# A planner for a fused attention and mixer kernel: one server for all DMAs, the weights' subtraction on DVE, and more of the work planned

## The chip, the core and the metric

The kernel runs on one core of a Trainium2 chip. A core has five engines that run side by side: TensorE (PE in the profile; its weight loads are PEld), VectorE (DVE), ScalarE (ACT), GpSimd (POOL) and SyncE (SP), which here only issues DMAs. Each engine works through its own instructions in the order in which they were written, and waits at one whose inputs or buffers aren't ready. The metric is the device time of one execution in microseconds.

## The reference

```python
scores = cap * np.tanh(scale * np.matmul(q, k.transpose(0, 1, 3, 2)) / cap)
attn = np.exp(scores - np.max(scores, axis=-1, keepdims=True))
attn = attn / (np.sum(attn, axis=-1, keepdims=True) + 1e-09)
x = np.matmul(attn, v)          # 4 batches, 12 heads, 448 tokens, 64 per head
x = x.transpose(0, 2, 1, 3).reshape(4, 448, 768)
h = np.maximum(x.transpose(0, 2, 1) @ w_tok1, 0.0) @ w_tok2      # 448 -> 256 -> 448
u = x + h.transpose(0, 2, 1)
out = u + np.maximum(u @ w_ch1, 0.0) @ w_ch2                     # 768 -> 1536 -> 768
```

The weights come as 64-bit floats, everything else as 32-bit floats.

## The kernel before

**Attention.** The heads are taken in pairs (24 pairs, 6 for each batch), and a pair in units: three blocks of 128 keys each, and the last 64 keys of two pairs together. A unit's scores are a product into bank pair ps_qk, ACT takes tanh (L334) and exp (L342) of them into a tile e, and a second product adds e times v to bank ps_pv. DVE adds the e tiles up (acc, L403, L410, L420). For two pairs at a time, a quad, PE sums acc over the keys (ps_s, L432); the sums go through SBUF (xs), four small DMAs (sums), a reciprocal on DVE (L471), a DMA to memory (rs) and four broadcasting DMAs (rb), and DVE multiplies the unscaled result by rb (L499) into u.

**Token mixing.** A half batch at a time: PE transposes u (ps_t, L508); ACT and DVE split the result in a high and a low part (L515, L518, L519); PE multiplies with w_tok1 (ps_h, 11 matmuls a tile, L536); ACT and DVE take the relu and split it (L542, L545); PE multiplies with w_tok2 (ps_u, 6 matmuls a tile, L559), and DVE adds it to u (L565). The tiles ps_s, ps_t, ps_h and ps_u share a ring of two banks, "c".

**Channel mixing.** u is split in high and low parts (ACT L655, DVE L656). For 6 groups of 256 of the 1536 channels and for each batch, `ch1` makes ps_g (36 matmuls, L771), whose relu is split by ACT (L779) and DVE (L780) into g; `ch2` makes six tiles ps_o (6 matmuls each, L796), and DVE adds each to u (L801). The tiles ps_o lie in rings "b" and "c" by turns.

**Weights.** A chunk of 512 columns is loaded as 64-bit numbers (wraw, L194, two buffers) and turned into a high and a low part: ACT takes a scaled absolute value (L212), DVE builds the 32-bit number from the bits (L218, L219, L225, L226), ACT rounds the high part (L235), and POOL subtracts it to get the low part (L239). Token weights are 4 chunks, each group of channel weights is 6, 36 in all; two sets of buffers alternate between groups.

**The order.** The order of the instructions on every engine is set by a planner that runs while the program is built. A `Job` has an engine, a cost (how long the engine is taken), a time to its result, and what it waits for; `Plan` gives each engine the job whose inputs are ready first, plus a slack by which less urgent work steps back. PE's own time is `plan.pe`. Token mixing is cut in steps that `background` puts between the attention units, a fixed quota of time after every second unit. DMAs are jobs on "sp" with a fixed time to landing each. Splits of u, the relu of `ch1` and the additions of `ch2` are written out in place, and the plan's clocks are moved along by hand. From the end of attention on, in `open_m1`, the hand-made order is closed.

## Time and profile before

| | |
|---|---|
| median of 3 runs | 605.88 us (605.72 to 608.96) |
| profiled execution, its time | 607.8 us |
| its span, first to last instruction | 605.7 us |
| mean granted clock of TensorE | 0.997 of 2.4 GHz |
| PE busy | 594.7 us |
| DVE busy | 388.0 us |
| ACT busy | 254.0 us |
| POOL busy | 57.6 us |

A busy time is the union of an engine's instructions. For PE it is no measure of how near it is to its peak, since matmuls overlap and their ends are modelled; what PE loses shows in its waits and in the clock that it was granted.

### The profile page before, as it was taken

How to read it: one execution, taken by the hardware profiler on the slowest of the kernel's cores; microseconds unless marked ns; L12 is line 12 of the kernel's file. 1: busy time of each engine (PE TensorE's matmuls, PEld its weight loads, DVE VectorE, ACT ScalarE, POOL GpSimd, SP SyncE). 2: the span in 40 equal slices, each digit the busy share in tenths (PEclk: the TensorE clock that was granted, in tenths of full speed). 3: DMA queues.
4: the chain of work that ended last, by engine and by line, in shares of the span. 5: the costliest groups of instructions: out<-in, count | busy, mean ns of one | idle time of the engine just before them, and what ended most of it. 6: DMA issues, size and time to landing. Idle time of an engine off the chain costs nothing.

```text
span 605.7 us, 7785 instructions
## 1 busy us (share of the span) xinstructions
PE 594.7 (98%) x3012; PEld 439.4 (73%) x3012; DVE 388.0 (64%) x626; ACT 254.0 (42%) x330; POOL 57.6 (10%) x48
## 2 busy tenths in 40 slices
PE   8999989999999999999999999999999999999997
PEld 2333434544454468888998999899999999999986
DVE  2999799967756787769685386437643753333324
ACT  7999877959685862342321022012211220000000
POOL 0201002110000000022310022002200120000000
PEclk9999989999999999999999999999999999999999
DMA  7534564414332023012323022202120200000224
GB/s 236 181 95 154 163 191 133 138 46 123 82 118 83 25 87 102 1 41 65 111 97 104 1 63 55 92 0 77 65 69 1 69 1 1 1 1 4 106 80 180
DMA packets 24621, 49.13 MB, mean 81 GB/s; under 512 B 6784, under 2 KB 16512, under 8 KB 24576
## 3 DMA queue, kind: packets, MB, share of 16 engines
q1 hardware_dynamic: 24288, 48.37, 25.5%
q8 instruction: 25, 0.41, 0.3%
q14 instruction: 20, 0.16, 0.1%
q10 hardware_dynamic: 288, 0.18, 0.1%
HBM read 42.86 MB, written 5.59 MB: 80 GB/s over the span
## 4 chain that ended last, share of the span: by engine, by line
PE 81%; DVE 12%; DMA 3%; issue 2%; ACT 2%; POOL 0%; SPq 0%; DVEq 0%; ACTq 0%; POOLq 0%
PE ps_o L796 27%; PE ps_g L771 25%; PE ps_pv L382 9%; PE ps_qk L312 8%; PE ps_u L559 3%; PE ps_h L536 3%; DVE wz L225 2%; PE ps_s L432 2%; DMA rb<-rs 2%; PE ps_qk L318 2%; PE ps_pv L385 1%; PE ps_t L508 1%; DVE wz L226 1%; DVE wz L219 1%; DVE uhl L656 1%
## 5 line engine op out<-in xcount | busy, mean ns | idle before, releaser
L796 PE MATMUL ps_o<-g,wc 128*128 128x448 f32 x864 | 181.8, 367 | 1.3 <-DVE u L801 1.0
L796 PEld LDWEIGHTS ps_o<-g,wc 128*128 128x128 f32 x864 | 161.5, 188 | 17.4 <-DVE u L801 2.5
L771 PE MATMUL ps_g<-uhl,wc 128*128 128x448 f32 x648 | 137.1, 367 | 0.0
L771 PEld LDWEIGHTS ps_g<-uhl,wc 128*128 128x128 f32 x648 | 121.1, 188 | 10.4
L801 DVE TENSOR_TENSOR u<-u,ps_o 128x448 f32<-128x448 f32 (+1 forms) x145 | 86.4, 613 | 46.3 <-PE ps_o L796 46.2
L334 ACT ACTIVATE e<-ps_qk,tsc 128x896 f32<-128x896 f32 x84 | 81.0, 1014 | 32.5 <-PE ps_qk L312 27.9
L239 POOL TENSOR_TENSOR wc<-wz,wc 128x512 fp32r<-128x512 f32 x36 | 49.3, 1372 | 396.5 <-ACT wc L235 371.3
L342 ACT ACTIVATE e<-e,near 128x896 f32<-128x896 f32 x84 | 84.4, 1051 | 0.0
L779 ACT ACTIVATE g<-ps_g 128x896 fp32r<-128x896 f32 x24 | 22.0, 915 | 144.8 <-PE ps_g L771 144.8
L780 DVE SCALAR_TENSOR_TENSOR g<-ps_g,g 128x896 fp32r<-128x896 f32 x24 | 26.1, 1088 | 74.4 <-ACT g L779 74.4
L312 PE MATMUL ps_qk<-qkraw 64*128 64x448 f32 x288 | 67.1, 575 | 0.2 <-DMA qkraw<-in_qk 0.2
L382 PE MATMUL ps_pv<-e,vn 128*64 128x448 f32 x288 | 64.9, 564 | 1.0 <-ACT e L342 1.0
L235 ACT ACTIVATE wc<-wz 128x512 fp32r<-128x512 f32 x36 | 22.6, 628 | 84.4 <-DVE wz L226 36.4
L312 PEld LDWEIGHTS ps_qk<-qkraw 64*128 64x128 f32 x288 | 24.4, 189 | 43.4 <-issue 18.2
L771 PE MATMUL ps_g<-last_u,wc 128*128 128x448 f32 x216 | 45.1, 366 | 1.4 <-issue 1.4
L771 PEld LDWEIGHTS ps_g<-last_u,wc 128*128 128x128 f32 x216 | 40.5, 188 | 5.2 <-issue 1.8
L212 ACT ACTIVATE wz<-wraw 128x512 f32<-128x512 f32 x36 | 24.1, 672 | 44.4 <-DMA wraw<-in_wc 25.1
L218 DVE TENSOR_SCALAR wz<-wz 128x512 f32<-128x512 f32 (+1 forms) x40 | 17.0, 428 | 38.0 <-ACT wz L212 37.9
L382 PEld LDWEIGHTS ps_pv<-e,vn 128*64 128x64 f32 x288 | 17.0, 137 | 32.6 <-issue 18.6
L403 DVE TENSOR_TENSOR acc<-e 128x896 f32<-128x896 f32 x24 | 26.2, 1091 | 19.0 <-ACT e L342 18.8
L420 DVE TENSOR_TENSOR acc<-acc,e 64x448 f32<-64x448 f32 x48 | 32.8, 683 | 6.4 <-ACT e L342 5.1
L536 PEld LDWEIGHTS ps_h<-wc,last_u 128*128 128x128 f32 x176 | 30.3, 188 | 9.0 <-issue 6.0
(50 smaller groups left out, 432.3 us busy)
## 6 DMA issues: line engine op xcount, KB each, us to landing
wraw<-in_wc SPq DMA_DIRECT2D x36, 512.0 KB, 3.5
qkraw<-in_qk SPq DMA_DIRECT2D x23, 448.0 KB, 3.6
vn<-in_v SPq DMA_DIRECT2D x24, 224.0 KB, 2.6
rb<-rs SPq DMA_DIRECT2D x48, 112.0 KB, 2.9
out_t<-u SPq DMA_DIRECT2D x23, 224.0 KB, 1.9
wraw<-in_w SPq DMA_DIRECT2D x2, 512.0 KB, 5.6
wraw<-in_w SPq DMA_DIRECT2D x2, 448.0 KB, 4.3
sums<-xs SPq DMA_DIRECT2D x48, 1.8 KB, 1.8
```

The costliest lines, as they stand in the source:

```text
L239: nc.gpsimd.tensor_tensor(lo, bits(held["z"]), hi, op=ALU.subtract)
L312: nc.tensor.matmul(ps[:, j, :S], raw[r, 1, c * P:(c + 1) * P], raw[r, 0], start=True, stop=True)
L334: nc.scalar.activation(e, ps[:, :, :S], AF.Tanh, scale=tsc)
L342: nc.scalar.activation(e, e, AF.Exp, scale=near)
L382: nc.tensor.matmul(o, vn[x % 3][:, j * NF + c], es[b, p, c][:, j], start=first, stop=last)
L403: nc.vector.tensor_tensor(accs[b, q][0][:, i], es[b, p, 0], es[b, p, 1], op=ALU.add)
L420: nc.vector.tensor_tensor(t, t, es[b, p - i, NF][r, i], op=ALU.add)
L536: nc.tensor.matmul(ps[:, :HALF], w, x, start=(n == 0), stop=(n == len(mm) - 1))
L771: nc.tensor.matmul(ps[:, i, :S], w[:, wi, cc, fs], uhl[b][:, ui, cc, :], start=(n == 0), stop=(n == 3 * NC - 1))
L780: nc.vector.scalar_tensor_tensor(g[:, 1], ps[:, :, :S], 0.0, g[:, 0], op0=ALU.max, op1=ALU.subtract)
L796: nc.tensor.matmul(ps[:, :S], w[:, wi, i, cs], g[:, gi, i, :], start=(n == 0), stop=(n == 3 * GF - 1))
L801: nc.vector.tensor_tensor(u[b][:, cc, r], u[b][:, cc, r], ps[:, r], op=ALU.add)
```

## The change

The planner's DMA jobs become transfers through one server: each has a size, the server works them off one after the other in the order of issue, at `BYTE` ns per byte, and a transfer lands `LANDING` ns after the server is done with it. The loads of the first channel weights get starting times that rise along the chunks. The subtraction of every decoded chunk goes from POOL to DVE. Splits of u, relu of `ch1` and additions of `ch2` become jobs of the plan; `ch2` takes a bank from the ring that comes free first; the first group's products are placed by a loop of their own (`first_group`) among what is left of token mixing; the quota of background work that wasn't used is kept for later, up to twice the quota; later groups' weights step back further (slack 60000 for 3000).

```diff
+LANDING = 1270
+BYTE = 3.8 / 1024
+STAGGER = 26.0
+SHARE = 7.0
+SPLIT = 2000.0
+SMALL = 8 * 1024
...
         at, e, j = n
         self.jobs[e].remove(j)
         self.free[e] = at + j.cost
-        j.end = at + j.took
+        if e == "sp":
+            self.bus = max(self.bus, self.free[e]) + j.took * BYTE
+            j.end = self.bus + LANDING
+        else:
+            j.end = at + j.took
         j.emit()
...
-            held["wz"].read(job("pool", 1400, 1400, last, (*key, 4), slack=slack, key=key))
+            held["wz"].read(job("dve", 530, 620, last, (*key, 4), slack=slack, key=key))
 
         def last():
-            nc.gpsimd.tensor_tensor(lo, bits(held["z"]), hi, op=ALU.subtract)
+            nc.vector.tensor_tensor(lo, bits(held["z"]), hi, op=ALU.subtract)
...
-        l = job("sp", 434, 3700, load, room("wraw"), since, slack=slack)
+        l = job("sp", 434, 8 * P * n, load, room("wraw"), since, slack=slack)
...
-        job("sp", 373, 3600, lambda: load_pair(b, p), room("raw"), slack=1500.0, key=("raw", b, p))
+        job("sp", 373, 8 * P * S, lambda: load_pair(b, p), room("raw"), slack=1500.0, key=("raw", b, p))
...
-        job("sp", 638, 2900, lambda: bring(0), m, room("rb"))
+        job("sp", 638, 8 * D * S, lambda: bring(0), m, room("rb"))
...
-    w0, w0_steps = group_weights(0, slack=20000.0, since=60000.0)
+    w0, w0_steps = group_weights(0, slack=20000.0, since=65000.0, stagger=STAGGER)
...
-        background(TOK / 7)
+        credit = min(credit + QUOTA, 2 * QUOTA)
+        credit -= background(credit)
...
-    def split_u(b, cc):
+    def split_u(b, slack=0.0):
...
+            job("act", 468, 568, high, ("u", b, cc), plan.pe, slack=slack, key=("uh", b, cc))
+            job("dve", 536, 620, low, ("uh", b, cc), slack=slack, key=("split", b, cc))
...
+        hold.read(job("act", 891, 918, high, plan.pe + DRAIN, slack=-500.0, key=("gh", g, b)))
+        hold.read(job("dve", 1010, 1092, low, ("gh", g, b), slack=-500.0, key=("g", g, b)))
...
-            pool, tag = ((ps_b, "b"), (ps_c, "c"))[cc % 2]
-            ps = pool.tile([P, 512], F32, tag=tag, name="ps_o")
+            clear(lambda: rings["b"].room() is None and rings["c"].room() is None)
+            n, tag = min((free_at(tag), tag) for tag in ("b", "c"))
+            plan.pe = max(plan.pe, n)
+            ps = (ps_b if tag == "b" else ps_c).tile([P, 512], F32, tag=tag, name="ps_o")
...
-            hold.read(plan.inline("dve", 530, 612))
+            hold.read(job("dve", 530, 612, lambda cc=cc, ps=ps: add_out(b, cc, ps, last), plan.pe + DRAIN))
...
+    def first_group(w):
+        started, g, at = 2, [], []
+        while len(g) < B:
+            if opened and started == 2:
+                started = 3
+            if started == 3 and not any(left):
+                done["tok",] = plan.pe
+                order.close()
+                split_tile(B - 1, None)
+                split_u(B - 1, -500.0)
+                started = B
+            n, m = len(g), len(at)
+            t = plan.ready([("split", n, 0)]) if n < started and n - m < 2 else None
+            if t is not None and t <= plan.pe + PATIENCE:
+                g.append(ch1(w[0], n))
+            elif m < n and (t := plan.ready([("g", 0, m)])) is not None and t <= plan.pe + PATIENCE:
+                ch2(w[1], m, g[m], False)
+                at.append(plan.pe)
+            elif not chunk():
+                rest()
+            fill()
```

What this does to the order is seen in three places. The first is SP's queue where the rb of batch 0's third quad are issued (line numbers differ, since the change adds lines: L194 is now L205, L286 is L298, L291 is L303, L462 is L477, L489 is L504). Before:

```order
L475 DMA rs<-sums 128x14
L291 DMA vn_96<-in_v 128x448
L194 DMA wraw<-in_wc 128x1024 x2
L286 DMA qkraw<-in_qk 128x896
L489 DMA rb<-rs 64x1x448 x4
L462 DMA sums<-xs 32x1x14 x4
```

Now:

```order
L490 DMA rs<-sums 128x14
L303 DMA vn_96<-in_v 128x448
L504 DMA rb<-rs 64x1x448 x4
L298 DMA qkraw<-in_qk 128x896
L205 DMA wraw<-in_wc 128x1024
L477 DMA sums<-xs 32x1x14 x4
L490 DMA rs<-sums 128x14
L504 DMA rb<-rs 64x1x448 x4
```

The q/k load and the weight load have moved behind the four rb, one weight load has gone from here altogether, and the next quad's sums, rs and rb follow.

The second place is DVE at the end of token mixing, where the last batch's u (u_78) is split into last_u while batch 1's additions of ps_o to u_76 begin. Before:

```order
L565 TENSOR_TENSOR u_78<-u_78,ps_u 128x448
L656 TENSOR_TENSOR last_u<-u_78,last_u 128x448 x3
L780 SCALAR_TENSOR_TENSOR g<-ps_g,g 128x896
L801 TENSOR_TENSOR u_76<-u_76,ps_o 128x448 x2
L656 TENSOR_TENSOR last_u<-u_78,last_u 128x448
L801 TENSOR_TENSOR u_76<-u_76,ps_o 128x448
```

Now:

```order
L581 TENSOR_TENSOR u_78<-u_78,ps_u 128x448
L676 TENSOR_TENSOR last_u<-u_78,last_u 128x448 x5
L237 SCALAR_TENSOR_TENSOR wz<-wraw,wz 128x512
L250 TENSOR_TENSOR wc_1_81<-wz,wc_1_81 128x512
L250 TENSOR_TENSOR wc_1_82<-wz,wc_1_82 128x512
L815 SCALAR_TENSOR_TENSOR g<-ps_g,g 128x896
L844 TENSOR_TENSOR u_76<-u_76,ps_o 128x448 x2
```

All splits now come ahead of the relu's low part (L815), together with two of the subtractions that were POOL's (L250).

The third place is PE in the first third of attention, at the second quad's sums (ps_s) and at the first token products (ps_h). Before, with other attention units left out between the two pieces:

```order
L312 MATMUL ps_qk<-qkraw 128x448 x4
L432 MATMUL ps_s<-acc,ones 32x448 x4
L382 MATMUL ps_pv<-e,vn_96 64x448 x2
...
L432 MATMUL ps_s<-acc,ones 32x448 x4
L536 MATMUL ps_h<-wc_1_81,last_u 128x384 x11
L382 MATMUL ps_pv<-e,vn_97 64x448 x4
L312 MATMUL ps_qk<-qkraw 128x448 x4
L536 MATMUL ps_h<-wc_1_81,last_u 128x384 x11
```

Now:

```order
L324 MATMUL ps_qk<-qkraw 128x448 x4
L394 MATMUL ps_pv<-e,vn_96 64x448 x2
L397 MATMUL ps_pv<-e,vn_96 64x448 x2
L397 MATMUL ps_pv<-e,vn_97 64x448 x2
L324 MATMUL ps_qk<-qkraw 128x448 x4
L445 MATMUL ps_s<-acc,ones 32x448 x4
L524 MATMUL ps_t<-ident,u_75 128x128 x4
...
L445 MATMUL ps_s<-acc,ones 32x448 x4
L552 MATMUL ps_h<-wc_1_81,last_u 128x384 x22
```

The sums have moved behind the next products and stand directly before a transpose; the 22 token products stand in one piece.

## Rows read from the trace of the kernel before

**Rows 1.** The page, busy time of the engines: us (share of the span) xinstructions
```profile
PE 594.7 (98%) x3012; PEld 439.4 (73%) x3012; DVE 388.0 (64%) x626; ACT 254.0 (42%) x330; POOL 57.6 (10%) x48
```
**Rows 2.** Who PE waited for: us in total, times, longest us
```profile
PE ps_t L508 <- DVE wc L545: 1.5, 1, 1.5
PE ps_g L771 <- issue: 1.4, 1, 1.4
PE ps_pv L382 <- ACT e L342: 1.0, 2, 0.9
PE ps_o L796 <- DVE u L801: 1.0, 1, 1.0
...
PE ps_h L536 <- DVE wc L519: 0.5, 1, 0.5
PE ps_u L559 <- DVE wc L519: 0.4, 1, 0.4
PE ps_o L796 <- DVE wc L519: 0.3, 1, 0.3
```
**Rows 3.** Stretches: length, busy PE, PEld, DVE, ACT, POOL, granted clock, DMA share, GB/s
```profile
20.00:40.00 20.00, 20.00 (x108) 5.70 (x106) 19.47 (x32) 20.00 (x23) 4.41 (x3) 1.00 0.48 151
...
80.00:82.00 2.00, 2.00 (x8) 0.57 (x8) 1.95 (x4) 2.00 (x4) 0.00 (x0) 0.54 1.02 280
82.00:84.00 2.00, 2.00 (x8) 0.69 (x6) 1.53 (x3) 0.24 (x1) 0.00 (x0) 0.61 1.02 286
```
**Rows 4.** Timeline of SP's queue from 63 us: start, length, instruction
```profile
63.93 0.81 SPq L194 DMA_DIRECT2D wraw<-in_wc  x2
64.80 0.42 SPq L286 DMA_DIRECT2D qkraw<-in_qk  x1
65.26 2.82 SPq L489 DMA_DIRECT2D rb<-rs  x4
```
**Rows 5.** DMA issues: count, KB each, median us from issue to landing
```profile
wraw<-in_wc SPq DMA_DIRECT2D x36, 512.0 KB, 3.5
qkraw<-in_qk SPq DMA_DIRECT2D x23, 448.0 KB, 3.6
...
rb<-rs SPq DMA_DIRECT2D x48, 112.0 KB, 2.9
```
**Rows 6.** Timeline from 72 to 79 us: DVE and PE, in brackets the idle time before
```profile
72.67 1.27 DVE L499 TENSOR_TENSOR u<-xr,rb 128x448 f32<-128x448 f32 x2 [2.67 <-DMA rb<-rs]
...
76.26 0.69 DVE L226 SCALAR_TENSOR_TENSOR wz<-wraw,wz 128x512 int32<-128x512 int32 x1
...
77.87 0.55 DVE L545 SCALAR_TENSOR_TENSOR wc<-ps_h,wc 128x384 fp32r<-128x384 f32 x1
...
78.48 0.66 PE L508 MATMUL ps_t<-ident,u 128*128 128x128 f32 x4 [1.45 <-DVE wc L545]
```
**Rows 7.** POOL's groups by form: count | busy us, mean ns | idle before
```profile
L239 POOL TENSOR_TENSOR wc<-wz,wc 128x512 fp32r<-128x512 f32 x36 | 49.3, 1372 | 396.5 <-ACT wc L235 371.3 <-issue 14.0 <-PE ps_o L796 7.3
L239 POOL TENSOR_TENSOR last_u<-wz,last_u 128x512 fp32r<-128x512 f32 x2 | 4.1, 2054 | 24.4 <-DVE last_u L233 24.4
```
**Rows 8.** DVE's groups by form, the same columns
```profile
L225 DVE SCALAR_TENSOR_TENSOR wz<-wraw,wz 128x512 int32<-128x512 int32 x38 | 32.9, 868 | 0.7
...
L226 DVE SCALAR_TENSOR_TENSOR wz<-wraw,wz 128x512 int32<-128x512 int32 x38 | 29.6, 781 | 0.8
...
L656 DVE TENSOR_TENSOR uhl<-u,uhl 128x448 fp32r<-128x448 f32 x18 | 10.5, 618 | 0.8 <-ACT uhl L655 0.7
```
**Rows 9.** Timeline from 277 to 282 us, DVE and PE
```profile
277.23 2.79 DVE L656 TENSOR_TENSOR last_u<-u,last_u 128x448 fp32r<-128x448 f32 x3
...
281.60 2.71 PE L796 MATMUL ps_o<-g,wc 128*128 128x448 f32 x12 [1.01 <-DVE u L801]
```
**Rows 10.** Timeline from 38 to 41 us, PE
```profile
38.14 1.98 PE L432 MATMUL ps_s<-acc,ones 128*32 128x448 f32 x8
...
40.05 0.97 PE L382 MATMUL ps_pv<-e,vn 128*64 128x448 f32 x4
```

More of the change, by code (lines that the diff above doesn't have):

```diff
@@ L101, in job @@
     def job(self, engine, cost, took, emit, *deps, slack=0.0, key=None):
-        j = Job(cost, took + SIGNAL, emit, deps, slack)
+        j = Job(cost, took if engine == "sp" else took + SIGNAL, emit, deps, slack)
         self.jobs[engine].append(j)
@@ L434, in add_rows @@
         of.read(plan.pe)
+        todo["attention"] -= 1
         def take():
@@ L451, in evac @@
         xr[b, p] = x
+        todo["attention"] -= 1
         holds["xr", b, p] = rings["xr"].take(1)
@@ L566, in add @@
             left[b] -= 1
-        hold.read(job("dve", 530, 615, add, plan.pe + DRAIN))
+        hold.read(job("dve", 530, 615, add, plan.pe + DRAIN, key=("u", b, cc)))
     TOK = 2 * (NHALF * 4 * 108 + NT * 11 * 174 + NHALF * 3 * NT * 203)
@@ L624, in background @@
     def background(ns):
-        while ns > 0:
-            c = chunk()
-            if not c:
-                return
-            ns -= c
+        spent = 0.0
+        while spent < ns and (c := chunk()):
+            spent += c
+        return spent
     def rest():
@@ L650, in split_tile, with one, high, low @@
         uhl[b] = t.rearrange("p (x c s) -> p x c s", x=2, c=NC)
-    def split_u(b, cc):
-        assert not left[b] and not any(i == b for i, _ in xr)
+    def split_u(b, slack=0.0):
         t = uhl[b]
-        nc.scalar.activation(t[:, 0, cc], u[b][:, cc], AF.Copy)
-        nc.vector.tensor_tensor(t[:, 1, cc], u[b][:, cc], t[:, 0, cc], op=ALU.subtract)
-        plan.free["act"] = max(plan.free["act"], plan.pe) + 468
-        plan.free["dve"] = max(plan.free["dve"], plan.free["act"] + 170) + 536
+        def one(cc):
+            def high():
+                nc.scalar.activation(t[:, 0, cc], u[b][:, cc], AF.Copy)
+            def low():
+                nc.vector.tensor_tensor(t[:, 1, cc], u[b][:, cc], t[:, 0, cc], op=ALU.subtract)
+            job("act", 468, 568, high, ("u", b, cc), plan.pe, slack=slack, key=("uh", b, cc))
+            job("dve", 536, 620, low, ("uh", b, cc), slack=slack, key=("split", b, cc))
+        for cc in range(NC):
+            one(cc)
     pairs = [(b, p) for b in range(B) for p in range(H // 2)]
@@ L751, in open_m1 @@
         nonlocal m1
-        clear(lambda: accs or pvp)
-        order.close()
+        clear(lambda: todo["attention"])
         e_att.close()
@@ L756, in open_m1, with await_time, await_key @@
         split_tile(1, m1)
+        split_u(1, SPLIT)
+    def await_time(of):
+        clear(lambda: of() is None)
+        plan.pe = max(plan.pe, of())
+    def await_key(key):
+        await_time(lambda: plan.ready([key]))
     def await_weights(name, g, i):
-        key = (name, g), i // DU * DU
-        clear(lambda: plan.ready([key]) is None)
-        plan.pe = max(plan.pe, plan.ready([key]))
+        await_key(((name, g), i // DU * DU))
     def ch1(w, b, g=0):
+        await_time(rings["a"].room)
         ps = ps_a.tile([P, 2, 512], F32, tag="a", name="ps_g")
+        hold = rings["a"].take(2)
         for i in range(GF):
@@ L793, in ch2, with add_out, free_at @@
             for i in range(GF):
[L794 removed]
+                await_weights("wc2", g, i * C + cc * P)
                 for wi, gi in ((0, 0), (1, 0), (0, 1)):
[L796 removed]
+                    nc.tensor.matmul(ps[:, :S], w[:, wi, i, cs], x[:, gi, i, :], start=(n == 0), stop=(n == 3 * GF - 1))
                     n += 1
[L798 to L803 removed]
             plan.spend(6 * 204)
[L805 removed]
+            hold.read(job("dve", 530, 612, lambda cc=cc, ps=ps: add_out(b, cc, ps, last), plan.pe + DRAIN))
             fill()
[L808 removed]
+    def add_out(b, cc, ps, last):
+        end = last and b == B - 1 and cc == NC - 1
+        for i, q in enumerate((nc.sync, nc.scalar) if end else (nc.sync,)):
+            r = slice(i * S // 2, (i + 1) * S // 2) if end else slice(0, S)
+            nc.vector.tensor_tensor(u[b][:, cc, r], u[b][:, cc, r], ps[:, r], op=ALU.add)
+            if last:
+                q.dma_start(out[b, :, cc, r], u[b][:, cc, r])
+    def free_at(tag):
+        t = rings[tag].room()
+        return float("inf") if t is None else t
+    opened = []
+    def fill():
+        if m1 is None and not todo["attention"]:
+            open_m1()
+        if m1 is not None and not opened and not todo["scale"]:
+            opened.append(open_m2())
+            split_u(2, SPLIT)
         plan.advance(plan.pe)
@@ L891, in general @@
             settle()
-        for k in [k for k in done if k[0] in ("x", "xh", "h", "hh", "t1", "t2")]:
+        for k in [k for k in done if k[0] in ("x", "xh", "h", "hh", "t1", "t2", "u", "uh", "split", "gh", "g")]:
             del done[k]
```

111 lines of the change are left out of this document (50 added, 61 removed).

## The prediction

> **What bounds the kernel now.** I read the page's list of engines first, then who PE waited for, then the clock by stretches, then the timeline at the places named there. PE is busy for 594.7 of 605.7 us; DVE for 388.0, ACT for 254.0, POOL for 57.6 [rows 1]. So the matmuls set the time, the change removes none of them, and what it can win is what PE loses. There are two kinds of loss. One is waits: the view of PE's waits holds 1.5 + 1.4 + 1.0 + 1.0 + 0.5 + 0.4 + 0.3 us in its larger rows [rows 2]. The other is a stretch at the lower clock, which the waits don't show: from 80 to 82 us the granted clock was 0.54 and from 82 to 84 us 0.61 of 2.4 GHz, so part of that time ran at 1.2 GHz [rows 3]. Compared with full speed that is 0.46 x 2 + 0.39 x 2 = 1.7 us of work lost. What the engine did before it fell: it had just stood still for 1.45 us [rows 6].
>
> Where that wait comes from can be followed backwards. The transposes of tile ps_t at 78.48 us waited for a DVE instruction of line 545, which ran only at 77.87 [rows 6]. DVE executes in the written order, and earlier it had stood for 2.67 us in front of line 499, waiting for tile rb [rows 6]. The DMAs of rb were issued from 65.26 us on, and on the same queue just ahead of them stood two weight loads (63.93 us) and a q/k load (64.80) [rows 4]: 2 x 512 + 448 = 1472 KB in front of 4 x 112 KB [rows 5]. An rb lands a median 2.9 us after its issue [rows 5]; here DVE got going at 72.67, 7.4 us after the first issue. That is a traffic jam which the planner didn't see: it let all six weight loads of group 0 start at 60 us and priced each DMA as if it were alone.
>
> **The change part by part.** *One server for DMAs, loads spread.* In the new order on SP these four rb stand ahead of the q/k load and of the first weight load, and the second weight load comes after the next four rb. What is left ahead of them is one v load (128x448 numbers, half a q/k load, 224 KB). At the rate seen while the engines were full, 280 GB/s [rows 3], 1472 KB take some 5.4 us and 224 KB 0.8; so these rb land about 4.5 us earlier relative to their issue and DVE's 2.67 us go. Would the transposes then go on without a wait? Line 545 at 77.87 less 2.67 is 75.2, plus its 0.55 is 75.8; PE was ready at 78.48 - 1.45 = 77.0. There is 1.2 us to spare, so both the wait of 1.45 and the 1.7 us of half clock go: **-3.2 us**. Next to be late would be the sums of the fourth quad, since their four small DMAs now stand behind a q/k load and a weight load: 960 KB, 3.5 us by the same rate. What is queued behind their reciprocal on DVE is the decode of the first weights, which nobody awaits soon; I give it no price here and take it up as a rival.
>
> *Subtraction on DVE instead of POOL.* 40 instructions, 36 for the channel weights [rows 7] and 4 for the token weights, go to DVE. No 128x512 subtraction of two SBUF tiles stands in DVE's rows. The nearest below is line 656, the same operation on 448 columns: 618 ns [rows 8]. The nearest of 512 columns with two SBUF tiles is line 226 at 0.69 us where POOL was idle [rows 6]. I take 0.69, as it has the width: 40 x 0.69 = 27.6 us more on DVE. Against that, DVE is slowed today while POOL subtracts: line 225 takes 868 ns on average and line 226 781 [rows 8], beside 0.69 alone. Over 38 instructions each that is 38 x (0.18 + 0.09) = 10.3 us given back. Net DVE gets 17 us more work by these two lines alone and less if others give back too. Rows and rule differ here: the Trainium skill, page "SBUF — State Buffer", section "SBUF: two separate sides", says that DVE and GpSimd take their shared pair of ports as an exclusive lock for a whole instruction, so that the later one blocks fully. By that rule up to POOL's whole 57.6 us could be DVE's gain, and DVE would end up 30 us lighter; I go by the rows. DVE has 605.7 - 388.0 = 218 us free, so the sum is the same with either: the net is hidden behind PE. The cover is missing only early: from 20 to 40 us DVE is busy for 19.47 of 20 us [rows 3]. There 4 moved subtractions cost 2.8 us and relieve DVE of four on POOL, two of them over 2 us long [rows 7]. I take that as even: **0**, with +2.8 us in front of the token products if nothing is relieved.
>
> *Splits, channel additions and group 0 planned.* The largest wait after attention, the branch apart, is 1.01 us at 281.60, where ps_o waited for an addition of line 801 that stood behind three splits. These took 2.79 us together [rows 9] where three of 0.618 take 1.9 [rows 8], because POOL subtracted at the same time. In the new order splits still stand there, but the slowing of 0.9 us is gone, and the matmuls take whichever of the two rings of banks frees first: **-1.0 us**. The smaller waits for DVE [rows 2] sum to 0.5 + 0.4 + 0.3 = 1.2 us; some come from the same slowing, some from the order. I take half: **-0.6**.
>
> *What stays.* The 1.4 us at "issue" [rows 2] is the branch near the end, which is untouched. The 1.0 us for ACT lies at 40 us, and ACT is busy for all of 20 to 40 us [rows 3], so it has no gap to give.
>
> *New waits.* A new order has waits of its own. I have followed PE's new order past its producers with the durations above and found none that must exceed half a microsecond, but the planner of before believed that of its order too. I allow **+0.8**, one wait of the kind that rows 2 hold.
>
> **Sum:** -3.2 - 1.0 - 0.6 + 0.8 = -4.0 us on the span, 605.7 to 601.7. The profiled execution took 607.8 us (2.1 around the span) and the median of the runs is 605.88, 1.9 below it. I take the difference off the median: 605.9 - 4.0 = **601.9 us**.
>
> **Rivals.** *A: another wait makes the clock fall.* At 38.14 us PE did the sums (ps_s) and then, after a wait of 1.0, an e product at 40.05 that needed an exponential [rows 2, 10]; the sums themselves are 40.05 - 38.14 - 1.0 = 0.9 us. In the new order they come later, so PE reaches the same product 0.9 us sooner and stands for 1.9. That is longer than the 1.45 us before the fall at 80 us. The wait itself is no loss, since the sums are done later where ACT is still the slower, but 1.7 us of half clock is: 603.6 us. Against it: the 1.0 us there left the clock alone, so length is not all. *B: the half clock isn't in the median.* The profile is 1.9 us above the median, near the 1.7 that I count for the clock; if the usual execution doesn't have it, the gain is 4.0 - 1.7 = 2.3 and the time again 603.6. One trace can't decide it. *C: no gain.* The jam only moves: the fourth quad's sums come 3.5 us late, and the chain of sums, reciprocal, rs and rb hands that to the next scaling, with as much stall as before. Then -1.6 and +0.8 are left: 605.1. *D: slower.* DVE is late early on. If POOL's slowing isn't given back, four subtractions put 2.8 us on DVE in the first 60 us and the six of group 0 another 4.1 up to 130 us, ahead of the results for which the 22 token products wait that now stand in one piece (11 and 11 before). It decides once DVE is later there than the 2.67 us that rb gives: 6.9 - 2.67 = 4.2 us of stall and another 1.7 of half clock, beside the 1.6 saved later and without the 3.2: 605.9 + 4.2 + 1.7 - 1.6 = 610.2. Against it: the stretched lines of rows 8.
>
> **How the numbers follow.** The forecast has 0.50 (599 to 602.8); A or B 0.24 (602 to 604.5), half of it under 602.9; C 0.16 (604 to 608.9); D 0.10. A measurement of this kernel can tell about 0.5%, 3 us: faster is below 602.9, slower above 608.9. So faster 0.50 + 0.12 = 0.62, the same 0.12 + 0.16 = 0.28, slower 0.10. Range: the low end is all waits for DVE gone (1.5 + 1.0 + 1.2), the clock's 1.7, no new wait, and 1.5 for gaps too short for that view: 605.9 - 6.9 = 599.0. The high end goes past C to 606.5, and leaves out D and C's upper part. The likeliest case alone is 599 to 602.8.
>
> **What would show it.** No wait of DVE over 1 us for rb between 60 and 85 us; granted clock 1.00 in every stretch from 10 us on; no ps_t wait over 0.3 there. POOL without subtractions, lines 225 and 226 (now 236 and 237) at 0.69 us everywhere, and DVE's busy time between 388 and 405 us. No wait of ps_o over 0.3 us between 240 and 300 us. I am wrong if PE's waits add up to as much as before at other places, above all at the 22 token products near 65 us or behind an rb after 70 us, or if a stretch at 1.2 GHz turns up near 40 us.

## The result and the profile after

The changed kernel takes 599.47 us (median of 4 executions, 599.39 to 599.75). Before, measured beside it, took 607.35 us (4 executions, 605.72 to 608.96). The ratio is 0.9871 with a 95% interval of 0.9836 to 0.9907, so the kernel is 1.3% faster. The profiled executions have spans of 605.7 us before and 598.0 us now, 7.7 us apart.

The page's list of engines, against [rows 1]: POOL is empty, DVE has 40 instructions more and is busy for 3.3 us more.

```profile
PE 590.1 (99%) x3012; PEld 440.0 (74%) x3012; DVE 391.3 (65%) x666; ACT 254.9 (43%) x330; POOL 1.1 (0%) x8
```

Who PE waited for, against [rows 2] (us in total, times, longest): of the waits for DVE one of 0.5 us is left, and the rest is the branch, the start-up and short waits for ACT and a load.

```profile
PE ps_g L802 <- issue: 1.3, 1, 1.3
PE ps_pv L394 <- ACT e L354: 0.8, 1, 0.8
PE ps_qk L324 <- DMA qkraw<-in_qk: 0.8, 1, 0.8
PE idle L702 <- PEq L1027: 0.8, 1, 0.8
PE ps_h L552 <- DVE wc L535: 0.5, 1, 0.5
PE ps_qk L330 <- ACT e L346: 0.4, 1, 0.4
```

Stretches, against [rows 3]: the granted clock is 1.00 where it was 0.54 and 0.61, although DVE is as full as before.

```profile
78.00:80.00 2.00, 2.00 (x11) 1.85 (x11) 1.97 (x4) 2.00 (x3) 0.00 (x0) 1.00 0.94 284
80.00:82.00 2.00, 2.00 (x12) 1.53 (x12) 1.97 (x4) 1.06 (x2) 0.00 (x0) 1.00 0.80 325
82.00:84.00 2.00, 2.00 (x12) 0.78 (x10) 1.99 (x4) 0.71 (x1) 0.00 (x0) 1.00 0.00 0
```

SP's queue where the third quad's rb are issued, against [rows 4]: as the new order said, rb goes out ahead of the q/k load and of the weight load.

```profile
62.64 2.40 SPq L504 DMA_DIRECT2D rb<-rs  x4
65.08 0.58 SPq L298 DMA_DIRECT2D qkraw<-in_qk  x1
65.71 0.43 SPq L205 DMA_DIRECT2D wraw<-in_wc  x1
```

DVE's forms, against [rows 8] (count | busy us, mean ns): the lines that took 868 and 781 ns take 686 and 689, and the subtraction (L250) takes 685 where I had taken 690.

```profile
L237 DVE SCALAR_TENSOR_TENSOR wz<-wraw,wz 128x512 int32<-128x512 int32 x38 | 26.2, 689 | 0.9
L236 DVE SCALAR_TENSOR_TENSOR wz<-wraw,wz 128x512 int32<-128x512 int32 x38 | 26.1, 686 | 0.5
L250 DVE TENSOR_TENSOR wc<-wz,wc 128x512 fp32r<-128x512 f32 x36 | 24.6, 685 | 19.0 <-ACT wc L246 18.1 <-PE ps_h L552 0.8
```

Waits and clock don't show everything, so I also worked out **what PE loses** from the starts of the matmuls: the time of a stretch less the count of matmuls times their steady distance at the full clock (204.4 ns for ps_g, ps_o and ps_u, 174 for ps_h, 108.5 for ps_t, 187.5 for the products of attention). Half clock, waits and changes between kinds of product all count in it. A matmul may fall on either side of an edge, and each figure is from one profile: the changed kernel and two kernels below that do the same up to 255 us (c_late, c_g1) have 0.9, 0.5 and 1.6 in the first stretch and 0.2, 0.5 and -0.3 in the second. So differences well under a microsecond say little. The first 60 us are left out, since the first loads land up to a microsecond earlier or later from one execution to the next.

| us lost by PE | 60 to 100 | 100 to 220 | 220 to 300 | 300 to 560 |
|---|---|---|---|---|
| before | 4.1 | 1.2 | 2.9 | 0.2 |
| after | 0.9 | 0.2 | 0.0 | 0.4 |

So 3.2 us come from the place at 78 us, 2.9 from the end of token mixing and 1.0 from what lies between; most of what is missing from the 7.7 lies in the first 60 us. Of the 3.2, 1.7 are the half clock, which the profiled execution of before had from 80 to 84 us [rows 3]; at full clock before lost 2.4 there, and the place is worth 1.5.

### The profile page after: what moved, and what is told of

It reads as the page before. It is cut to its first block, busy times and chain, and to the rows that moved or that the text cites. A ratio compares the mean times of both kernels' runs of the same rounds, so it can differ in the third digit from the quotient of the medians.

```text
span 598.0 us, 7725 instructions
## 1 busy us (share of the span) xinstructions
PE 590.1 (99%) x3012; PEld 440.0 (74%) x3012; DVE 391.3 (65%) x666; ACT 254.9 (43%) x330; POOL 1.1 (0%) x8
## 4 chain that ended last, share of the span: by engine, by line
PE 89%; DVE 7%; DMA 2%; issue 1%; ACT 0%; SPq 0%; DVEq 0%
PE ps_g L802 30%; PE ps_o L834 30%; PE ps_pv L394 7%; PE ps_qk L324 7%; PE ps_h L552 5%; PE ps_u L575 5%; PE ps_t L524 2%; PE ps_qk L330 1%; DVE acc L433 1%; PE ps_pv L397 1%; PE ps_s L445 1%; DVE acc L423 1%; DMA wraw<-in_w 1%; DVE acc L416 1%; DMA qkraw<-in_qk 1%
## 5 line engine op out<-in xcount | busy, mean ns | idle before, releaser
L812 ACT ACTIVATE g<-ps_g 128x896 fp32r<-128x896 f32 x24 | 22.1, 923 | 148.2 <-PE ps_g L802 147.9
L815 DVE SCALAR_TENSOR_TENSOR g<-ps_g,g 128x896 fp32r<-128x896 f32 x24 | 26.1, 1088 | 78.6 <-ACT g L812 78.6
L250 DVE TENSOR_TENSOR wc<-wz,wc 128x512 fp32r<-128x512 f32 x36 | 24.6, 685 | 19.0 <-ACT wc L246 18.1
L552 PE MATMUL ps_h<-wc,last_u 128*128 128x384 f32 x176 | 33.9, 340 | 0.5 <-DVE wc L535 0.5
L575 PE MATMUL ps_u<-last_u,wc 128*128 128x448 f32 x144 | 33.0, 374 | 0.0
```

The source lines that it names most:

```text
L250: nc.vector.tensor_tensor(lo, bits(held["z"]), hi, op=ALU.subtract)
L552: nc.tensor.matmul(ps[:, :HALF], w, x, start=(n == 0), stop=(n == len(mm) - 1))
L575: nc.tensor.matmul(ps[:, :S], h1[:, hi, t, cs], w2s[:, wi, t, :], start=(n == 0), stop=(n == 3 * NT - 1))
L815: nc.vector.scalar_tensor_tensor(x[:, 1], ps[:, :, :S], 0.0, x[:, 0], op0=ALU.max, op1=ALU.subtract)
```

## The experiments

The change has three parts: DMAs (server, spread loads), the subtraction on DVE, and the plan (splits, channel additions, first group, saved quota). The last column shows what PE lost in the four stretches of the table above.

| kernel | DMAs | subtraction | plan | median us (executions) | ratio to before, 95% | lost by PE |
|---|---|---|---|---|---|---|
| p_dma | new | POOL | old | 607.18 (12) | 0.9993 (0.9978 to 1.0008) | 2.7, 1.9, 1.0, 2.9 |
| p_plan | old | POOL | new | 607.82 (12) | 0.9996 (0.9983 to 1.001) | 3.7, 1.8, 2.2, 1.2 |
| p_dve | old | DVE | old | 602.25 (6) | 0.9924 (0.9899 to 0.9948) | 0.4, 2.3, 1.2, 0.4 |
| u_pool | new | POOL | new | 603.67 (8) | 0.9921 (0.9895 to 0.9948) | 1.0, 0.4, 2.6, 1.3 |
| u_plan | new | DVE | old | 601.71 (6) | 0.9894 (0.9858 to 0.9929) | 0.8, 1.7, 0.4, 0.5 |
| u_dma | old | DVE | new | 601.70 (6) | 0.9892 (0.9858 to 0.9926) | 0.0, 2.3, 0.1, 0.4 |

Before was measured anew beside each set of kernels. Its median was 609.05 us beside u_pool, u_plan, u_dma and c_emit, 607.69 beside the p kernels and c_before_emit, and 606.98 beside the last four. Between sets, differences of a microsecond therefore say little. The changed kernel itself was measured in the first set only, so what undoing a part cost is given by the medians and, more safely, by the ratios to before (0.9871 for the changed kernel): 4.2 and 3.0 us for u_pool, 2.2 and 1.3 for u_plan and u_dma, 3.8 and 2.6 for c_emit. For u_plan and u_dma the intervals overlap widely with that of the changed kernel.

### One part undone

**u_pool** gives the subtraction back to POOL, for the planner too.

```diff
-            held["wz"].read(job("dve", 530, 620, last, (*key, 4), slack=slack, key=key))
+            held["wz"].read(job("pool", 1400, 1400, last, (*key, 4), slack=slack, key=key))
...
-            nc.vector.tensor_tensor(lo, bits(held["z"]), hi, op=ALU.subtract)
+            nc.gpsimd.tensor_tensor(lo, bits(held["z"]), hi, op=ALU.subtract)
```

> The changed kernel with one edit undone: the subtraction of a decoded chunk goes back to POOL, and the planner again counts 1400 ns of POOL for it; everything else as changed. Theory S (a relief of DVE counts only where something waits for DVE): what comes back is the 0.9 us of slowed splits at the end of token mixing and some tenths in attention, so 600.3 to 601.5 us, with lines 236 and 237 again at 780 to 870 ns on average and DVE's busy time at most 5 us from the 391.3 of the changed kernel, since its 27 us of subtractions leave and the slowing of 24 us returns. Theory L (DVE's slowing is what costs most of the 7.7 us): 603 us or more, with PE losing again around 70 to 80 us. Theory N (nobody waits for DVE): 599.2 to 599.8.

Measured: 603.67 us. That is theory L's time, but not at its place: 60 to 100 us lost 1.0 as in the changed kernel, while 220 to 300 us lost 2.6 and 300 to 560 us 1.3. The timeline of u_pool near 290 us shows how (POOL's, DVE's and PE's rows; in brackets the idle time before):

```profile
287.40 0.43 DVE L230 TENSOR_SCALAR wz<-wz 128x512 int32<-128x512 int32 x1
287.57 1.41 POOL L250 TENSOR_TENSOR wc<-wz,wc 128x512 fp32r<-128x512 f32 x1 [2.49 <-ACT wc L246]
287.86 1.67 DVE L236 SCALAR_TENSOR_TENSOR wz<-wraw,wz 128x512 int32<-128x512 int32 x1
289.45 1.08 DVE L815 SCALAR_TENSOR_TENSOR g<-ps_g,g 128x896 fp32r<-128x896 f32 x1
290.45 1.14 DVE L844 TENSOR_TENSOR u<-u,ps_o 128x448 f32<-128x448 f32 x2
291.11 2.10 PE L834 MATMUL ps_o<-g,wc 128*128 128x448 f32 x9 [1.46 <-DVE u L844]
```

Line 236 comes 0.3 us after POOL has begun and ends at 289.53, 0.55 us after POOL has ended at 288.98. It waited out the whole of POOL's instruction. Behind it stand the relu's low part (L815, at 289.45; at 285.14 in the changed kernel) and the additions that free the banks, and PE stands for 1.46 us. About 1 us of the 4.3 by which the relu's low part is later is this one wait; the rest is the other order and what was late before it.

**u_plan** is the kernel before with the new DMAs and the subtraction on DVE; **u_dma** is the changed kernel with fixed landing times and all loads of group 0 from 60 us on (its diff is the first hunks of the change, and the last of these lines, backwards).

```diff
-        l = job("sp", 434, 8 * P * n, load, room("wraw"), since, slack=slack)
+        l = job("sp", 434, 3700, load, room("wraw"), since, slack=slack)
...
-    w0, w0_steps = group_weights(0, slack=20000.0, since=65000.0, stagger=STAGGER)
+    w0, w0_steps = group_weights(0, slack=20000.0, since=60000.0)
```

> The kernel before with the server for DMAs, the spread loads and the subtraction on DVE, but splits of u, relu of ch1 and additions of ch2 written out in place as before, two rings by turns, no loop of its own for the first group, no saved quota, slack 3000 for later weights. Theory S: attention runs as in the changed kernel, and of the 2.9 us that PE gained between 220 and 300 us, what the hand-written order costs comes back, 1.5 to 2.5 us: 601.0 to 602.0 us, with waits of ps_o or ps_g for DVE over 0.3 us there. Rival L: the transition was slow because POOL slowed DVE there; then it is gone without the planned splits too: 599.3 to 600.2 us.

Measured: 601.71 us, theory S's time for another reason. Between 220 and 300 us PE lost only 0.4; the rest lies between 100 and 220 us (1.7), spread over short gaps. With POOL idle the hand-written transition loses next to nothing, as rival L said.

> The changed kernel with fixed landing times for DMAs again and all six pairs of weight loads of group 0 from 60 us on; the subtraction on DVE and the planned splits stay. In its order two weight loads, a v load and a q/k load stand ahead of four rb near 65 us, as before. Theory S: the jam is back: DVE stands 2 us or more before a scaling, the transposes wait 1 us or more, and the clock may fall again: 601.5 to 603 us. Rival L: the jam cost time only because DVE was slowed by POOL as well; with the subtraction on DVE the transposes wait less than 0.4 us: 599.3 to 600.3 us, whatever DVE waits for rb.

Measured: 601.70 us, theory S's time again, and again not its cause. From 60 to 100 us PE lost 0.0, and DVE's longest wait for rb there was 0.72 us. The loss of 2.3 us sits before 220 us. ACT's and PE's timelines of u_dma there:

```profile
215.58 2.91 ACT L669 ACTIVATE uhl<-u 128x448 fp32r<-128x448 f32 x6
218.38 0.59 ACT L527 ACTIVATE wc<-ps_t 128x512 fp32r<-128x512 f32 x1
218.86 1.04 ACT L350 ACTIVATE e<-e,near 128x896 f32<-128x896 f32 x1
...
217.37 1.46 PE L571 MATMUL ps_u<-last_u,wc 128*128 128x448 f32 x6 [0.55 <-DVE wc L531]
219.96 0.97 PE L390 MATMUL ps_pv<-e,vn 128*64 128x448 f32 x4 [1.12 <-ACT e L350]
```

Six splits of batch 0 were put on ACT ahead of the exponential that the last products of attention need. This is a matter of the order that the other times led to, and not of a late transfer.

### The plan untouched, and only the subtraction's engine changed

**c_emit** keeps the changed kernel's plan; **c_before_emit** keeps before's. That holds the order fixed only as long as the hand-made order lasts. In before it is closed at the end of attention, in the changed kernel at the end of token mixing (`order.close()`); from there on the order is made by the framework that builds the program, and it comes out otherwise. The subtractions apart, DVE's instructions stand in the same order in c_emit and the changed kernel up to 260 us, and in c_before_emit and before up to 264 us; behind that some are exchanged.

```diff
# c_emit, against the changed kernel
-            nc.vector.tensor_tensor(lo, bits(held["z"]), hi, op=ALU.subtract)
+            nc.gpsimd.tensor_tensor(lo, bits(held["z"]), hi, op=ALU.subtract)
# c_before_emit, against the kernel before
-            nc.gpsimd.tensor_tensor(lo, bits(held["z"]), hi, op=ALU.subtract)
+            nc.vector.tensor_tensor(lo, bits(held["z"]), hi, op=ALU.subtract)
```

> The changed kernel with the planner's order untouched (it still believes in 530 ns of DVE), but the subtraction itself is given to POOL. It measures what POOL does to DVE with the order held fixed. Theory L: lines 236 and 237 go from 686 and 689 to about 870 and 780 ns, and other DVE lines with two SBUF tiles or 32-bit integers stretch too, so that DVE's busy time falls by well under the 27 us of subtractions that leave it (0 to 8 us); the time is 600 to 602.5 us. Rival: the slowing of before came from the order, and DVE's lines stay below 720 ns; DVE is 27 us lighter and the time 599.2 to 599.8 us.

Measured: 603.25 us (8 executions, 602.12 to 605.03; ratio 0.9913, 0.9883 to 0.9942), 3.8 us above the changed kernel, a little beyond theory L's range. PE lost 1.2, 0.2, 2.3 and 1.4 us in the four stretches: as long as the order is the same, next to nothing, and behind it all of the loss. The page's engines, and two of DVE's forms in c_emit:

```profile
PE 592.1 (98%) x3012; PEld 439.4 (73%) x3012; DVE 391.1 (65%) x626; ACT 254.2 (42%) x330; POOL 55.4 (9%) x48
```

```profile
L236 DVE SCALAR_TENSOR_TENSOR wz<-wraw,wz 128x512 int32<-128x512 int32 x38 | 32.0, 842 | 0.7
L230 DVE TENSOR_SCALAR wz<-wz 128x512 int32<-128x512 int32 x38 | 23.9, 630 | 1.0
```

The same instructions, less 40 that are worth 27.2 us in the changed kernel, keep DVE busy for 391.1 us instead of 391.3. While POOL subtracts, DVE loses by being held up all that it was spared.

PE's longest wait for DVE in c_emit shows what a hold costs where DVE is awaited:

```profile
288.37 1.41 POOL L250 TENSOR_TENSOR wc<-wz,wc 128x512 fp32r<-128x512 f32 x1 [2.21 <-ACT wc L246]
288.66 1.66 DVE L236 SCALAR_TENSOR_TENSOR wz<-wraw,wz 128x512 int32<-128x512 int32 x1
290.25 1.08 DVE L815 SCALAR_TENSOR_TENSOR g<-ps_g,g 128x896 fp32r<-128x896 f32 x1
291.25 1.14 DVE L844 TENSOR_TENSOR u<-u,ps_o 128x448 f32<-128x448 f32 x2
291.91 2.71 PE L834 MATMUL ps_o<-g,wc 128*128 128x448 f32 x12 [1.29 <-DVE u L844]
```

DVE has no gap between these rows, the relu's high part had left ACT (L812) at 289.03, and line 236 takes 0.97 us longer than the 0.69 that it takes without POOL. So 0.97 of the 1.29 us is the hold, whatever the order. How the rest of the loss behind 260 us divides between holds, the other order and the subtraction's own length (1.3 to 1.4 us on POOL for 0.69 on DVE; ACT stood 17.8 us for it, 9.8 in the changed kernel) no run separates.

> The kernel before with its order of instructions untouched; only the subtraction is emitted on DVE where it was emitted on POOL, and the planner goes on counting it for POOL. The DMAs are issued in the old order, so the jam stays. Theory J: DVE still stands 2 us or more for rb near 70 us, the transposes still wait 1 us or more, and the clock can still fall; what is won is in the transition: 603.5 to 606 us. Rival K: with DVE's instructions at 690 ns again the transposes wait less than 0.5 us: 601.5 to 603.5 us. In both, lines 225 and 226 go to 686 ns. Beside it a theory D: the planner doesn't know of the 40 new DVE instructions, and they stand in front of something that PE awaits: no gain at all, 606 us or more.

Measured: 605.08 us (12 executions; ratio 0.9968, 0.9949 to 0.9986), 2.6 us less than before. The jam stays and the time is in theory J's range, though neither wait reaches its 1 us. DVE's and PE's timelines:

```profile
71.31 1.20 DVE L499 TENSOR_TENSOR u<-xr,rb 128x448 f32<-128x448 f32 x2 [2.15 <-DMA rb<-rs]
...
77.05 0.66 PE L508 MATMUL ps_t<-ident,u 128*128 128x128 f32 x4 [0.86 <-DVE wc L545]
78.51 0.63 PE L508 MATMUL ps_t<-ident,u 128*128 128x128 f32 x4 [0.81 <-DVE wc L519]
```

The wait of 1.45 us [rows 6] is now two, of 0.86 and 0.81. Eight of the 12 executions have a mean granted clock of 0.993 to 0.997 and four of 0.999 to 1.000, so the half clock is there more often than before. With POOL gone and the order unchanged, the place at 78 us isn't better: PE lost 3.0 us between 60 and 100 us in a profile with a mean clock of 0.999, and before lost 2.4 there without its half clock. Between 100 and 220 us it lost 2.2 instead of 1.2. What can be seen of the gain lies between 220 and 300 us, 1.7 instead of 2.9.

### One part alone, on the kernel before

**p_dma** has the server and the spread loads, **p_dve** the subtraction on DVE, **p_plan** the rest. Of each one line stands here; the others are those of the change.

```diff
# p_dma
-    w0, w0_steps = group_weights(0, slack=20000.0, since=60000.0)
+    w0, w0_steps = group_weights(0, slack=20000.0, since=65000.0, stagger=STAGGER)
# p_dve
-            held["wz"].read(job("pool", 1400, 1400, last, (*key, 4), slack=slack, key=key))
+            held["wz"].read(job("dve", 530, 620, last, (*key, 4), slack=slack, key=key))
# p_plan
-            hold.read(plan.inline("dve", 530, 612))
+            hold.read(job("dve", 530, 612, lambda cc=cc, ps=ps: add_out(b, cc, ps, last), plan.pe + DRAIN))
```

> The kernel before with the server for DMAs and the spread loads alone. Theory J (the jam in front of rb is the whole cause of the wait at 78 us): DVE's 2.67 us before the scaling go, the transposes don't wait, the granted clock stays 1.00 between 76 and 86 us, and the time falls by 3.2 us against executions of before that have the clock's fall, by 1.5 against those without: 603.5 to 605.5 us; between 220 and 300 us PE loses as much as before. Rival K (the jam met a DVE that POOL had already made late): a wait of 1 us or more for DVE is left somewhere between 60 and 90 us, and the time is within 1 us of before.

Measured: no difference from before (607.18 against 607.69 us), which is rival K's time. The wait at 78 us has gone, and none of the 12 executions has a clock below 0.999, as theory J said. But others took its place. Who PE waited for in p_dma:

```profile
PE ps_o L806 <- DVE u L811: 2.2, 2, 1.3
PE ps_pv L392 <- ACT e L352: 1.2, 2, 0.9
PE ps_h L546 <- DVE u L575: 1.1, 1, 1.1
```

The 1.1 us end at 94.22 us; a little earlier, at 88.85, DVE's line 430 (two sums of acc) took 2.31 us, where the two took 1.25 at 78.50, because POOL subtracted from 89.41 on. The 2.2 us stand at 308 and 325 us, where weights of a later group are decoded: both times line 234 was held by POOL shortly ahead of the relu's low part (1.66 us from 304.81 and 1.74 from 321.69).

> The kernel before with the subtraction on DVE, and planned there (530 ns of DVE for 1400 of POOL); DMAs, loads, splits and channel additions as before. From what undoing this edit cost the changed kernel (603.67 against 599.47 us), 3 to 4 us are expected from it here too if the parts add up: 602 to 605 us. If the parts don't add up because the hand-written order at the end of token mixing is the next limit there, 1 us or less: 605 to 608 us.

Measured: 602.25 us, 5.4 us less than before by this one edit, where 3 to 4 were expected. The planner, told of 530 ns of DVE instead of 1400 of POOL, issues two weight loads at 58.91 us, still ahead of the rb (65.69), and DVE waits 0.82 and 0.87 us for these, but PE only 0.4 for ps_t.

> The kernel before with splits, relu, channel additions and first group planned, the saved quota and the larger slack, but subtraction on POOL, fixed landing times, and all loads from 60 us on. Undoing this part cost the changed kernel 2.2 us. If the parts add up: 2 us under before, 603.5 to 607 us. Rival L: while POOL slows DVE the plan's times at the end of token mixing are wrong by up to 1 us an instruction, and the planned order loses there what the written one loses: within 1 us of before.

Measured: 607.82 against 607.69 us, no difference, as rival L said. Its longest wait of ps_o for DVE is 1.2 us, and 60 to 100 us loses 3.7 us.

### Which of the subtractions cost

**c_g1** and **c_late** keep the changed kernel's plan and emit 6 or 24 of the 40 subtractions on POOL (those of channel group 1; those of groups 2 to 5). Here too DVE's order is the changed kernel's only up to 260 us (c_g1) and 287 us (c_late).

```diff
-            nc.vector.tensor_tensor(lo, bits(held["z"]), hi, op=ALU.subtract)
+            late = key[0][1:] and key[0][1] == 1
+            (nc.gpsimd if late else nc.vector).tensor_tensor(lo, bits(held["z"]), hi, op=ALU.subtract)
```

In c_late the condition is `>= 2`.

> The changed kernel, order untouched, with 6 of its 40 subtractions emitted on POOL: those of channel group 1, which fall between 255 and 300 us. With all 40 on POOL the time was 603.25 us, and beyond 599.47 the larger part (2.2 us) was lost between 260 and 300 us. Theory P (POOL's slowing of DVE costs where PE awaits DVE): these six cost about 2.2 us: 601.2 to 602 us, with a wait of ps_o for DVE over 1 us near 290 us. Rival E (every subtraction on POOL costs the same, by its length): 6 of 40 times 3.8 is 0.6: 599.9 to 600.3 us.

> The changed kernel, order untouched, with the 24 subtractions of channel groups 2 to 5 emitted on POOL. Theory P: from 300 us on almost nothing waits for DVE; the run with all 40 on POOL lost 1.0 us there: 600.0 to 600.7 us. Rival E: 24 of 40 times 3.8 is 2.3: 601.5 to 602 us. In both, DVE's lines 230, 236 and 237 stretch in these groups.

Measured beside each other: c_g1 601.41 us (4 executions; ratio 0.9912, 0.9896 to 0.9929), c_late 599.54 (4; 0.9888, 0.9866 to 0.9909). By the medians of four the six cost 1.9 us more than the 24 (one execution of c_late has 601.28), and between 220 and 300 us PE lost 1.9 us in c_g1 and 0.2 in c_late; the 24 cost nothing that can be measured, less even than theory P had given them. The wait at 290 us was 0.72 us, less than I had expected, with another of 0.6 for ps_u before it. The page of c_late, where POOL is busy for 32.9 us and PE loses nothing by it:

```profile
PE 590.5 (99%) x3012; PEld 439.7 (74%) x3012; DVE 389.7 (65%) x642; ACT 254.1 (43%) x330; POOL 32.9 (6%) x32
```

There 24 instructions fewer, 16 us of work, spare DVE 1.6 us; so it was held for some 15 us and PE lost nothing. The length of the slowing is not what costs. Rival E is out by over 1 us for the one and 2 for the other. That the six cost by their holds alone, as theory P has it, isn't shown. The wait of 0.6 for ps_u in c_g1:

```profile
259.61 1.07 DVE L229 TENSOR_SCALAR wz<-wz 128x512 f32<-128x512 f32 x1 [0.46 <-ACT wz L223]
261.48 0.68 DVE L236 SCALAR_TENSOR_TENSOR wz<-wraw,wz 128x512 int32<-128x512 int32 x1
262.08 0.61 DVE L582 TENSOR_TENSOR u<-u,ps_u 128x448 f32<-128x448 f32 x1
262.75 0.47 PE L576 MATMUL ps_u<-last_u,wc 128*128 128x448 f32 x1 [0.57 <-DVE u L582]
```

Line 229 was held for 0.64 us, but line 236 also stands ahead of the addition that PE awaits, where it stood behind it in the changed kernel. And ahead of the wait at 290 us the last subtraction on POOL had ended 9 us before. Hold and order act together here.

### The two halves of the DMA part

**u_server** takes the server out of the changed kernel and keeps the spread; **u_spread** does the reverse.

```diff
# u_server
-        if e == "sp":
-            self.bus = max(self.bus, self.free[e]) + j.took * BYTE
-            j.end = self.bus + LANDING
-        else:
-            j.end = at + j.took
+        j.end = at + j.took
# u_spread
-    w0, w0_steps = group_weights(0, slack=20000.0, since=65000.0, stagger=STAGGER)
+    w0, w0_steps = group_weights(0, slack=20000.0, since=60000.0)
```

> The changed kernel with fixed landing times again, but the weight loads of group 0 still spread. Undoing both cost 2.2 us, and in that trace the loss lay not behind a late rb but near 218 us, where splits of batch 0 stood on ACT ahead of an exponential that PE awaited. Theory W (the spread loads are what keeps rb free; the server only changes a few places in the order): 599.4 to 600.2 us. Rival V (the server's times are what the planner needs to place work at the end of attention): 601.2 to 602.2 us with a wait of PE for ACT or DVE of about 1 us between 200 and 225 us.

> The changed kernel with the server, but all weight loads of group 0 wanted from 60 us on, without spreading. Theory W: two weight loads stand ahead of the third quad's sums, reciprocal and rb, and DVE waits for rb or sums 1 us or more between 65 and 85 us: 600.5 to 602 us. Rival V: the server sees the loads coming and puts other work first: 599.4 to 600.2 us, and DVE's wait costs PE nothing.

Measured: u_server 601.06 us (4 executions, 599.47 to 601.11; ratio 0.9896, 0.9877 to 0.9915), u_spread 600.28 (4, 599.69 to 601.73; ratio 0.9900, 0.9880 to 0.9919). With spreads of that size, and c_late at 599.54 beside them, neither half is clearly worth more than a microsecond by itself, and the two theories are not told apart by the times. Nor by their signs: in u_server PE has no wait of half a microsecond between 200 and 225 us, and in u_spread DVE none for rb between 60 and 85 us. But u_spread decides another question. DVE's timeline, and PE's in the same place:

```profile
154.69 0.63 DVE L514 TENSOR_TENSOR u<-xr,rb 128x448 f32<-128x448 f32 x1 [5.39 <-DMA rb<-rs]
...
149.09 1.72 PE L394 MATMUL ps_pv<-e,vn 128*64 128x448 f32 x8
150.75 1.77 PE L324 MATMUL ps_qk<-qkraw 64*128 64x448 f32 x8
152.45 0.97 PE L552 MATMUL ps_h<-wc,last_u 128*128 128x384 f32 x4
153.26 0.60 PE L524 MATMUL ps_t<-ident,u 128*128 128x128 f32 x4
153.79 0.97 PE L394 MATMUL ps_pv<-e,vn 128*64 128x448 f32 x4
154.69 0.98 PE L397 MATMUL ps_pv<-e,vn 64*64 64x448 f32 x8
155.60 1.77 PE L324 MATMUL ps_qk<-qkraw 64*128 64x448 f32 x8
157.31 1.09 PE L524 MATMUL ps_t<-ident,u 128*128 128x128 f32 x8
```

DVE stood for 5.39 us in front of rb, twice as long as in [rows 6], and PE's products follow each other without a gap. A late rb is not a loss by itself.

## Why the prediction was right, and where it wasn't

The range held the time, by 0.5 us at its low end, and the direction was right; all the signs named under "What would show it" came. The sum was not right: -4.0 us, where the profiled spans differ by 7.7 and the time is 6.4 under the median of 605.88 that I had started from. That the range held is in part luck: its low end had been set for waits and gaps, with nothing for what the subtraction brought. Its terms one by one:

**The term of 0 for the subtraction is the one that failed.** "The sum is the same with either: the net is hidden behind PE" was its step, and both halves were wrong. The first was the size. I counted what two lines gave back, 10.3 us; all lines gave back some 27 (c_emit). The row that I had beside the rule, means of 868 and 781 ns, is a mix of instructions that POOL didn't hold up, at 690, and others at 1.2 to 1.8 us; so the rows did not differ from the rule, only their mean did. The Trainium skill, page "SBUF — State Buffer", section "SBUF: two separate sides", has the later one of DVE and GpSimd block for the whole instruction; line 236 in u_pool, which ended 0.55 us after POOL did, agrees. Its upper bound as I had used it (POOL's whole 57.6 us) was not reached: about half of that. The second half was the cover. "DVE has 218 us free" is a sum over the whole span; in front of the waits at 78 us (before) and 290 us (u_pool, c_emit) DVE had next to none. c_g1 and c_late show that six subtractions there cost 1.9 us, with the order that they bring, and 24 elsewhere nothing. Alone, this edit brings 5.4 us, and in the changed kernel's plan it is worth 2.6 us by the ratios and 3.8 by the medians (c_emit).

**The -3.2 at 78 us came out to the tenth (4.1 to 0.9) in these two profiles, for a cause that I had only half.** The jam was there, and rb did move ahead of it. But without the jam and with POOL subtracting, PE still lost 2.7 us there (p_dma), where before lost 2.4 besides its half clock; without POOL's subtractions but in the old order 3.0 (c_before_emit); with the subtraction off POOL and known to the planner 0.4, with no change to the DMAs (p_dve). Two things made DVE late, and removing either alone moved the loss to the next place. That is rival C, which would have been right of the DMA part by itself: it took away the half clock (none of 12 executions has it) and, by the median, little else.

**The -1.0 for the transition was mis-sized: 2.9.** I had followed one wait, 1.01 us behind the splits. There are several, and the costliest in u_pool and c_emit is behind the relu's low part. With the subtraction back on POOL 2.6 of the 2.9 return, with the splits and additions written out by hand 0.4; so beside the new DMAs this term belonged mostly to the subtraction, and the part of the change to which I had put it does little. With the old DMAs it does more (1.2 in p_dve, 0.1 in u_dma), and p_dma lost only 1.0 there with the subtraction on POOL and the old plan. So it depends on how the orders fall together, and no single part owns it.

**The -0.6 for small waits was 1.0**, and what makes it is not settled. In the kernels here the loss between 100 and 220 us goes from next to nothing (the changed kernel) to 3.0 (u_server) with the order, so it can't be laid to one edit.

**The +0.8 for new waits wasn't needed.** PE waits 0.46 us for the 22 token products, and not at all for the fourth quad's sums, before which DVE stood for 0.78.

**Rival A rested on a misread row.** The wait of 1.0 us for an exponential in [rows 2] is two, and the one of 0.9 lies at 10 us, in the start-up. PE's timeline of before there:

```profile
10.36 0.97 PE L382 MATMUL ps_pv<-e,vn 128*64 128x448 f32 x4 [0.85 <-ACT e L342]
```

At 38 us the sums themselves waited for DVE, 0.25 and 0.51 us by the rows of PE's weight loads, and that wait left with them. **Rival B was right of before.** In the three later sets 6 of 15, 8 of 29 and 0 of 7 executions of before have a mean granted clock of 0.998 or less. They have medians of 610.4 and 608.6 us where the others of their sets have 607.3 and 607.4. The fall of the clock is in about a quarter of the executions and goes with 1.2 to 3.1 us, so taking 1.7 us for it off a median of 605.88, beside which stand 605.72 and 608.96, probably counted it where it wasn't. By that the forecast was 603.6, and the subtraction made up for it. **Rival D** had DVE heavier by the subtractions; it isn't.

The parts don't add up, and that is the reason why "where did the gain go" has no answer part by part. DMAs alone and plan alone bring 0.5 and 0 us. The two together, still with POOL (u_pool), have a ratio of 0.9921; the subtraction alone has nearly the same, 0.9924; all three 0.9871.

## What to carry to other kernels

Before costing work on GpSimd as free, look at the longest of the DVE instructions that run beside it, not at their mean: if there are two heights a microsecond apart, one engine holds up the other, and the GpSimd time is to be counted on DVE. What a relief of an engine is worth is looked for in the few microseconds ahead of the waits for that engine; a share of the span, or a standstill in front of a DMA, says nothing of it. Undo parts in the presence of the others as well as adding them alone: here two of three parts are worth nothing alone and two microseconds or more together.

## What the runs showed of the hardware

Whether POOL holds up a DVE instruction depends on its operands and on which of the two began first. In c_emit, for the DVE instructions that overlap a POOL subtraction by more than 0.1 us (worked out from all rows of that trace; ns, counts in brackets):

```
line, operands                             without POOL   begun before    begun while
                                              (median)     POOL's began   POOL subtracts
L230  wz, one input in SBUF, 512 columns     427 (27)      426 to 428 (5)  1328 to 1470 (8)
L236  wraw and wz, two in SBUF, 512          688 (28)      676 to 693 (5)   901 to 1749 (7)
L237  wraw and wz, two in SBUF, 512          691 (35)       none           1256 to 1673 (5)
L433  acc and e, two in SBUF, 448            622 (41)      618 to 622 (3)  1153 to 1609 (4)
L844  u and ps_o, one of them in PSUM, 448   617 (135)     614 to 622 (8)   614, 616    (2)
```

The one that begins first isn't held up. The one that begins later ends a fixed time after POOL has ended, whenever it began: line 230 0.28 us, lines 236 and 237 0.55 (0.48 for the one with 448 columns, the 901 of the table), line 433 0.48. POOL is held up in the same way: its subtraction takes 1.29 us by itself, and 1.66 where line 236 had begun 0.16 us ahead of it. With one input in PSUM POOL is not felt: beside the two of line 844 there are ten such instructions in the trace of before that began while POOL subtracted (lines 450, 518, 519, 545, 565 and 801), all of the usual length. The Trainium skill, page "SBUF — State Buffer", section "SBUF: two separate sides", names as the instructions that take the shared ports those of DVE with two SBUF inputs or in a two-port mode; the table agrees, if line 230 runs in such a mode, as its 427 ns beside the 685 of line 250 for as many columns suggest.

The mean granted clock was 0.997 or less in eight of 12 executions of c_before_emit, where PE stood for 0.86 us and, 1.5 us later, for 0.81, and 0.998 or less in 14 of 51 of before, where it stood once for 1.45 in the profiled execution. In neither kernel did it come every time. The profiled execution of c_before_emit is one with 0.999, so where the clock falls in that kernel is not shown.
